# Chunked attention and a multiplicative FFN: the first pair turned by TensorE, its loads split over two queues, and a new order of the opening steps

## The chip, the cores and the metric

The kernel runs on one core of one Trainium2 chip. The metric is the device time of one execution in microseconds (us); the time before is the median of three runs. A profiled execution shows when each engine's instructions ran: TensorE (PE, with its weight loads PEld), VectorE (DVE), ScalarE (ACT), GpSimd (POOL) and SyncE (SP), and the loads and stores that they issue.

## The reference

Inputs q, k, v have the shape (8 batches, 8 heads, 576 positions, 64), in fp32. Attention stays inside chunks of 64 positions; its output feeds a feed-forward part (FFN) of 4608 tokens:

```python
scores = scale * np.matmul(q_c, k_c.transpose(0, 1, 2, 4, 3))      # 64x64 in each chunk
scores = scores - np.max(scores, axis=-1, keepdims=True)
attn = np.exp(scores)
attn = attn / (np.sum(attn, axis=-1, keepdims=True) + 1e-09)
out = np.matmul(attn, v_c)
x = out.transpose(0, 2, 1, 3).reshape(B * S, H * D)                # 4608 x 512
a = x @ w1                                                         # 512 -> 1024
b = x @ w2
h = a * b @ w3                                                     # 1024 -> 1024
return (h @ w_out).astype(np.float32)                              # 1024 -> 512
```

## The kernel before

**Tiling.** Tokens are worked off in 18 "pairs" p of 256 tokens (four chunks of 64); two pairs form a group g of 512 tokens. Everything is computed in bf16 with fp32 sums. The exponentials are taken without subtracting the maximum; at the end a check of the sums decides whether a slow second path has to run (it does not here). The two last matrices are multiplied once, w3·w_out (steps V, W, Z), so that the FFN is (a·b) times one 1024x512 matrix.

**An order written by hand.** The string `ORDER` lists every step of the kernel. The loop at the end of `first_path` runs through it and calls a function for each letter; `inorder` (L90) pins each instruction to its place in its engine's program. So each engine works through its own instructions in the order of the string, and waits for whatever the next of them needs. The steps:

- Loads through GpSimd's queue, cast to bf16 on the way (`load`, L97): `q p`, `k p`, `v p`; `i j`, a quarter of the columns of w1 and of w2; `h j`, a half of w3; `o`, w_out. Eight loads can be in flight; the ninth is issued when the first has landed. A pair whose four chunks lie in two batches is loaded in two pieces (`spans`, L119).
- `R s` (L135): raw fp32 q (s = 0, on SP's queue) and k (s = 1, on ScalarE's queue) of pair 0, in runs of 512 bytes. `K s` (L141): ScalarE casts them to bf16.
- `T p.s` (L195): VectorE transposes q or k of pair p in 32x32 blocks, so that the head dimension lies on the partitions. `G` and `H` (from pair 8 on) put such blocks in place with transfers on SP's queue.
- `S p`, `E p`, `P p` (L214, L231, L238): scores on TensorE, exp on ScalarE, product with v on TensorE. `N p.u` (L258): VectorE takes the reciprocal of the sums and normalises one half (128 tokens) of the pair. `X p.u` (L293): VectorE transposes that half into `xt`, the FFN's input.
- `A p.j`, `B p.j` (L342, L346): the FFN's two first products. For pairs 0 to 3 one such step is 8 matmuls of 256 columns for a quarter j of w1 (A) or w2 (B), so that it needs load `i j` alone. `C p.j` (L349): ScalarE copies A's result out of PSUM. `M p.j` (L353): VectorE multiplies it with B's.
- `V f`, `W m`, `Z m`: w3 transposed by VectorE, multiplied with w_out by TensorE, copied by ScalarE. `O p`, `Y p`, `Q p`: the last product of a pair, its copy and its store.
- `D` (L318): matmuls of zeros that nobody reads: which tile, how many, how many columns. `D0.0.0.16.64` is 16 matmuls of 64 columns; `D0.1.0.4.512` and `D1.0.0.5.512` are four and five of 512 columns, placed between the attention of pairs 0 and 1.

**Buffers.** PSUM is one pool of four tiles of two banks each (`psum`, L100); scores, P's two halves, an A/B step, W and O all take tiles from it, and a tile is free again when its last reader in the order is done (E, N, M, Z or Y). q and k of a pair are one tile of a pool of five; v has six buffers, pair p in buffer p modulo 6.

The opening of the order before the change, up to the first FFN steps:

```
R0 R1 v0 q1 k1 i0 v1 i1 i2 q2 k2 v2 i3 q3 k3 v3 q4 k4 v4 o h0 h1 D0.0.0.16.64 K0 T0.0 K1 T0.1 q5 k5
v5 S0 T1.0 E0 P0 D0.1.0.4.512 T1.1 q6 k6 v6 N0.0 S1 D1.0.0.5.512 X0.0 N0.1 X0.1 A0.0 E1 B0.0 C0.0 P1
```

Of the kernel before, what the change touches and what calls it, by code (L numbers as in the profile page):

```python
# [9 lines left out]
R0 R1 v0 q1 k1 i0 v1 i1 i2 q2 k2 v2 i3 q3 k3 v3 q4 k4 v4 o h0 h1 D0.0.0.16.64 K0 T0.0 K1 T0.1 q5 k5  # L10
v5 S0 T1.0 E0 P0 D0.1.0.4.512 T1.1 q6 k6 v6 N0.0 S1 D1.0.0.5.512 X0.0 N0.1 X0.1 A0.0 E1 B0.0 C0.0 P1
M0.0 A0.1 N1.0 X1.0 B0.1 C0.1 N1.1 A0.2 X1.1 B0.2 C0.2 M0.1 A1.0 T2.0 B1.0 C1.0 M0.2 A1.1 T2.1 q7 k7
v7 B1.1 C1.1 M1.0 S2 M1.1 A0.3 E2 T3.0 B0.3 C0.3 P2 M0.3 A1.2 N2.0 X2.0 B1.2 C1.2 N2.1 A1.3 X2.1
B1.3 C1.3 M1.2 A2.0 T3.1 q8 k8 v8 B2.0 C2.0 M1.3 S3 T4.0 A2.1 E3 M2.0 B2.1 T4.1 q9 k9 C2.1 P3 v9
M2.1 A2.2 N3.0 B2.2 C2.2 X3.0 A2.3 N3.1 B2.3 X3.1 C2.3 M2.2 S4 M2.3 A3.0 E4 B3.0 C3.0 A3.1 M3.0 B3.1
C3.1 V0 A3.2 M3.1 B3.2 C3.2 V1 A3.3 M3.2 B3.3 C3.3 V2 W0 M3.3 V3 W1 Z0 V4 V5 W2 Z1 V6 V7 T5.0 Z2 W3
T5.1 q10 k10 T6.0 T6.1 P4 v10 q11 k11 Z3 S5 N4.0 O0 E5 X4.0 N4.1 X4.1 T7.0 O1 T7.1 Y0 Q0 T8.0 P5 v11
q12 k12 Y1 S6 T8.1 O2 Q1 E6 N5.0 X5.0 N5.1 X5.1 O3 T9.0 T9.1 Y2 G4.0 P6 v12 q13 k13 A4.0 N6.0 B4.0
G4.1 Y3 X6.0 N6.1 C4.0 A4.1 X6.1 B4.1 C4.1 M4.0 Q2 S7 Q3 M4.1 A4.2 E7 T10.0 B4.2 C4.2 T10.1 P7 v13
q14 k14 A4.3 M4.2 B4.3 N7.0 C4.3 A4.4 X7.0 M4.3 B4.4 C4.4 N7.1 A4.5 M4.4 B4.5 C4.5 X7.1 S8 M4.5 S9  # L20
E8 A4.6 T11.0 B4.6 E9 T11.1 P8 v14 q15 k15 C4.6 A4.7 M4.6 G5.0 B4.7 C4.7 N8.0 A6.0 M4.7 B6.0 N8.1
# [12 lines left out]
A12.5 M12.4 B12.5 C12.5 A12.6 M12.5 B12.6 C12.6 A12.7 M12.6 B12.7 C12.7 O9 M12.7 O10 Y9 Q9 A14.0 Y10
B14.0 C14.0 Q10 A14.1 M14.0 B14.1 C14.1 A14.2 M14.1 B14.2 C14.2 A14.3 M14.2 B14.3 C14.3 A14.4 M14.3
B14.4 C14.4 A14.5 M14.4 B14.5 C14.5 A14.6 M14.5 B14.6 C14.6 A14.7 M14.6 B14.7 C14.7 O11 M14.7 O12
Y11 Q11 A16.0 Y12 B16.0 C16.0 Q12 A16.1 M16.0 B16.1 C16.1 A16.2 M16.1 B16.2 C16.2 A16.3 M16.2 B16.3
C16.3 A16.4 M16.3 B16.4 C16.4 A16.5 M16.4 B16.5 C16.5 A16.6 M16.5 B16.6 C16.6 A16.7 M16.6 B16.7
C16.7 O13 M16.7 O14 Y13 Q13 O15 Y14 Q14 O16 Y15 Q15 Y16 Q16 O17
# [7 lines left out]
def first_path(  # L47
# [66 lines left out]
    inorder(nc.vector.memset(zero[:], 0.0))  # L114
    vbuf = [consts.tile([P, 2, H, VW], bf, name=f"vbuf{i}") for i in range(6)]
# [19 lines left out]
    def do_R(s):  # L135

        raw_t[s] = msb.tile([P, H, 2 * D], f32, tag="o_sb", name="raw")
        inorder((nc.sync, nc.scalar)[s].dma_start(
            raw_t[s][:], (q, k)[s][0, :, 0:4 * CH, :].rearrange("h (p t) d -> p h (t d)", t=2)))

    def do_K(s):  # L141
        if 0 not in qk_t:
            qk_t[0] = io.tile([P, 2, H, 2 * D], bf, tag="qk", bufs=5, name="qk")
        inorder(nc.scalar.copy(qk_t[0][:, s], raw_t[s][:]))  # L144
# [19 lines left out]

    def load_v(p):
        for u in range(2):
            for at, b, c, m in spans(4 * p + 2 * u, 2):
                load(vbuf[p % 6][at * CH:(at + m) * CH, u, :, 0:D],
                     v[b, :, c * CH:(c + m) * CH, :].rearrange("h p d -> p h d"))
# [34 lines left out]

    def do_G(g, a):
# [52 lines left out]
    def do_N(p, u):  # L258
# [3 lines left out]
        if u == 0:  # L262
            xn_t[p] = asb.tile([P, 2, 2, 4, D], bf, tag="xn", bufs=3, name="xn")
# [304 lines left out]
```

## Time and profile before

| What | us |
|---|---|
| median of 3 runs (243.94 to 244.39) | 244.36 |
| span of the profiled execution, first to last instruction | 242.9 |
| TensorE busy in it | 226.7 |
| VectorE busy | 154.3 |
| ScalarE busy | 85.2 |
| GpSimd busy (issuing its loads, mostly) | 83.7 |
| first scores matmul (S0) | 9.82 |
| first FFN matmul (A0.0) | 16.57 |
| w3·w_out product done | 65.93 |

The page gives for each engine its busy time and, in 40 slices of the span, its busy share in tenths. A busy TensorE is not one at its peak, since matmuls are pipelined and the ends are modelled. The loads through GpSimd's queue are 18.9 MB in 82,592 packets. A releaser ("<-") behind a wait is the instruction or the transfer that ended it, as semaphore events tell; "issue" is a wait for nothing that the profile shows.

### The profile page before, as it was taken

The page shows a single profiled execution, that of the slowest core. Times are in us where ns is not written, and L with a number is a line of the kernel's source. Part 1 is how long each engine was busy: PE and PEld are TensorE (multiplying, and loading weights), DVE is VectorE, ACT ScalarE, POOL GpSimd, SP SyncE. Part 2 cuts the span into 40 slices and gives each one's busy share as a digit, 9 for nine tenths or more (in the row PEclk, how much of TensorE's full clock was granted, in tenths as well). Part 3 has the DMA queues.
Part 4 walks back from the last instruction along what each step waited for, and adds up shares of the span by engine and source line. Part 5 has one row for each costly group of instructions (what it writes and reads, how often), then busy time and mean ns, then how long its engine had stood idle before and what let it go on. Part 6 is the DMA issues. An engine that isn't in the chain of part 4 may idle for free.

```text
span 242.9 us, 6385 instructions
## 1 busy us (share of the span) xinstructions
PE 226.7 (93%) x2753; PEld 120.2 (49%) x2753; DVE 154.3 (64%) x235; ACT 85.2 (35%) x116; POOL 83.7 (34%) x114
## 2 busy tenths in 40 slices
PE   1189989999999999999999999999999999999994
PEld 1147868874445444444444444444444444444443
DVE  1756799699799588999998899918540332143000
ACT  2412423423333344425336234162332332322322
POOL 7856976656986345764160230000000000000000
PEclk9999999999999999999999999999999999999999
DMA  6999999999999999999999793735502200400244
GB/s 173 179 185 181 185 169 200 196 193 171 167 173 218 222 228 259 179 224 196 205 236 223 221 139 91 163 88 209 142 0 89 87 0 0 173 3 1 86 173 173
DMA packets 93597, 37.65 MB, mean 155 GB/s; under 512 B 75008, under 2 KB 86528, under 8 KB 93568
## 3 DMA queue, kind: packets, MB, share of 16 engines
q0 software_dynamic: 82592, 18.88, 83.9%
q1 hardware_dynamic: 9936, 17.83, 24.0%
q10 hardware_dynamic: 1040, 0.52, 0.8%
q8 instruction: 21, 0.34, 0.6%
q14 instruction: 8, 0.07, 0.1%
HBM read 38.80 MB, written 9.44 MB: 199 GB/s over the span
## 4 chain that ended last, share of the span: by engine, by line
PE 72%; DMA 16%; DVE 4%; SPq 3%; POOL 2%; issue 1%; ACT 0%; DVEq 0%; POOLq 0%
PE ab_ps L95 39%; PE o_ps L95 23%; PE w_ps L95 6%; DMA w<-in_moe_w_dram 4%; DMA qkm<-qkT 3%; SPq L193 3%; DMA qk<-in_q_dram 3%; DMA qk<-in_k_dram 3%; DMA xt<-xm 3%; PE pv L95 2%; PE s_ps L95 2%; DVE qkT L201 2%; POOL vbuf L98 1%; POOL w L98 1%; DVE xt L297 1%
## 5 line engine op out<-in xcount | busy, mean ns | idle before, releaser
L95 PE MATMUL ab_ps<-xt,w 128*128 128x512 bf16 (+1 forms) x688 | 127.4, 342 | 0.7 <-DVE xt L297 0.6
L95 PEld LDWEIGHTS <-w 128*128 128x128 bf16 x704 | 67.1, 98 | 56.1 <-issue 1.8
L366 DVE TENSOR_TENSOR ab<-a_sb,ab_ps 128x512 bf16<-128x512 f32 x71 | 47.8, 674 | 43.4 <-ACT a_sb L351 43.1
L351 ACT COPY a_sb<-ab_ps 128x512 f32<-128x512 f32 x71 | 41.6, 586 | 81.3 <-PE ab_ps L95 81.0
L95 PE MATMUL o_ps<-w3o,ab 128*128 128x512 bf16 (+1 forms) x296 | 63.9, 373 | 0.0
L201 DVE STREAM_TRANSPOSE qkT<-qk 128x1024 bf16<-128x1024 bf16 x36 | 45.1, 1291 | 7.2 <-ACT qk L144 5.5
L95 PEld LDWEIGHTS <-ab 128*128 128x128 bf16 x296 | 28.5, 98 | 32.2
L98 POOL DMA_DIRECT2D vbuf<-in_v_dram x40 | 33.9, 855 | 20.4 <-DMA qk<-in_q_dram 5.2
L396 ACT COPY o_sb<-o_ps 128x1024 f32<-128x1024 f32 x17 | 17.2, 1012 | 45.3 <-PE o_ps L95 41.3
L264 DVE TENSOR_TENSOR xn<-pv,rcs 128x512 bf16<-128x512 f32 x36 | 24.9, 692 | 1.4
L98 POOL DMA_DIRECT2D qk<-in_q_dram x23 | 18.1, 790 | 8.9 <-DMA qk<-in_k_dram 2.4
L98 POOL DMA_DIRECT2D qk<-in_k_dram x23 | 18.0, 783 | 6.5 <-DMA vbuf<-in_v_dram 3.7
L234 ACT ACTIVATE e<-s_ps 128x1024 bf16<-128x1024 f32 x16 | 15.9, 1026 | 1.7 <-PE s_ps L95 1.3
L95 PE MATMUL w_ps<-wo,w3T 128*128 128x512 bf16 x64 | 14.0, 379 | 0.0
L305 DVE STREAM_TRANSPOSE xm<-xn 128x512 bf16<-128x512 bf16 x20 | 13.5, 696 | 0.2
L261 DVE RECIPROCAL rcs<-pv 128x8 f32<-128x8 f32 x36 | 6.9, 193 | 10.4 <-PE pv L95 10.4
L98 POOL DMA_DIRECT2D w<-in_moe_w_dram x16 | 11.1, 695 | 5.3 <-DMA wo<-in_moe_w_out_dram 2.9
L95 PEld LDWEIGHTS <-e 64*32 64x32 bf16 (+1 forms) x832 | 7.8, 97 | 8.7 <-issue 6.9
L95 PE MATMUL pv<-vbuf,e 64*32 64x65 bf16 (+1 forms) x832 | 10.2, 197 | 1.8 <-ACT e L234 1.1
L297 DVE STREAM_TRANSPOSE xt<-xn 128x512 bf16<-128x512 bf16 x16 | 11.4, 711 | 0.5
L389 DVE COPY o_sb<-o_ps 128x256 f32<-128x256 f32 x1 | 0.4, 425 | 16.0 <-PE o_ps L95 16.0
L95 PEld LDWEIGHTS <-qkT 32*64 32x64 bf16 x512 | 5.5, 117 | 10.1 <-DVE qkT L201 7.9
(29 smaller groups left out, 54.2 us busy)
## 6 DMA issues: line engine op xcount, KB each, us to landing
out_dram<-o_sb SPq DMA_DIRECT2D x17, 512.0 KB, 3.3
qkm<-qkT SPq DMA_DIRECT2D x40, 128.0 KB, 4.0
vbuf<-in_v_dram POOLq DMA_DIRECT2D x32, 128.0 KB, 8.2
w<-in_moe_w_dram POOLq DMA_DIRECT2D x16, 256.0 KB, 9.9
qk<-in_q_dram POOLq DMA_DIRECT2D x11, 256.0 KB, 6.8
qk<-in_k_dram POOLq DMA_DIRECT2D x11, 256.0 KB, 7.8
xt<-xm SPq DMA_DIRECT2D x40, 64.0 KB, 3.2
wo<-in_moe_w_out_dram POOLq DMA_DIRECT2D x4, 256.0 KB, 7.1
```

The lines of the kernel that those rows point to most:

```text
L95: return inorder(nc.tensor.matmul(*a, **kw))
L98: return inorder(nc.gpsimd.dma_start(dst, src))
L193: inorder(nc.sync.dma_start(dst, src))
L201: inorder(nc.vector.transpose(qkT_t[g][:, :, p % 2, s, heads(h)].rearrange("p e h (y t) -> p h t e y", t=2), qk_t[p][:, s, heads(h)].rearr ...
L234: inorder(nc.scalar.activation(e_t[p][:, :, heads(hh)], s_t[p][:].rearrange("p u (h q) -> p u h q", q=CH)[:, :, heads(hh)], Exp, scale=sca ...
L261: inorder(nc.vector.reciprocal(rc, pv[:, :, :, D:W]))
L264: inorder(nc.vector.tensor_mul(xn_t[p][:, u], pv[:, :, :, 0:D], rc.to_broadcast([P, 2, 4, D])))
L297: inorder(nc.vector.transpose(new_xt(g)[:].rearrange("p (o t) -> p o t", o=KO)[:, :, t0:t0 + UT] .rearrange("p o (m y) -> p m o y", y=BL), ...
L305: inorder(nc.vector.transpose(xm_t[g][:, u, :, m].rearrange("p o (c y) -> p c o y", y=BL), xn_t[p][:].rearrange("p u r m d -> p (u r) m d" ...
L351: inorder(nc.scalar.copy(a_t[p, j][:], ps_t[p, j][:, 0, :]))
L366: inorder(nc.vector.tensor_mul(o, view(a_t.pop((p, j))[:]), view(ps_t.pop((p, j))[:, 1, :])))
L396: inorder(nc.scalar.copy(o_sb[:], ps_t.pop(p)[:]))
```

## The change

Six things change, and the rest of the kernel stays:

1. The raw q and k of pair 0 are loaded in runs of 1 KB: four positions of a head lie in one partition. Heads 0 to 3 go to partitions 0 to 63 on SP's queue, heads 4 to 7 to partitions 64 to 127 on ScalarE's queue; q first, then k.
2. The cast K is split into two halves, one on VectorE (`K s.0`) and one on ScalarE (`K s.1`).
3. Pair 0's q and k are transposed by TensorE (`t`, 8 transposes of 128x128 for each of q and k, against an identity matrix `eye` that GpSimd makes at the start) into PSUM, and copied out by `u`, two halves for each, one on VectorE and one on ScalarE. T0.0 and T0.1 are gone. Its x is transposed the same way (`y`, 4 transposes for each half, and `z`, a copy on ScalarE); X0.0 and X0.1 are gone.
4. With this layout S0 and P0 are 32 matmuls each (64 before), with 64 rows contracted in each. N0 orders its output for `y` and takes two products of 128x256 for each half.
5. v's buffers are taken from a list: a load takes the buffer that has been given back first, P gives it back.
6. The order is new from its start to about G4.0. In it pairs 0, 1 and 2 have their attention ahead of the first FFN steps (S2 S0 P0 S1 P2, then A0.1 B0.1 A2.1 P1), the loads go q2 k2 q1 k1 v0 v2 i1 v1 i0 q3 k3 i2 v3 i3 h0 o, the FFN steps go by quarters of the weights over three pairs, and only the first of the three groups of zero matmuls (D0.0.0.16.64) is left. From "C4.0 A4.1" on the order is the one of before.

```diff
-R0 R1 v0 q1 k1 i0 v1 i1 i2 q2 k2 v2 i3 q3 k3 v3 q4 k4 v4 o h0 h1 D0.0.0.16.64 K0 T0.0 K1 T0.1 q5 k5
-v5 S0 T1.0 E0 P0 D0.1.0.4.512 T1.1 q6 k6 v6 N0.0 S1 D1.0.0.5.512 X0.0 N0.1 X0.1 A0.0 E1 B0.0 C0.0 P1
-M0.0 A0.1 N1.0 X1.0 B0.1 C0.1 N1.1 A0.2 X1.1 B0.2 C0.2 M0.1 A1.0 T2.0 B1.0 C1.0 M0.2 A1.1 T2.1 q7 k7
...
+R0 R1 q2 K0.0 k2 K1.0 K0.1 D0.0.0.16.64 T2.0 t0.0 K1.1 u0.0.0 t0.1 T2.1 q1 u0.1.0 u0.1.1 T1.0 S2
+u0.0.1 S0 k1 v0 E0 T1.1 P0 v2 S1 N0.0 y0.0 E2 z0.0 i1 N0.1 P2 N2.0 N2.1 y0.1 z0.1 v1 X2.0 X2.1 i0
+A0.1 B0.1 E1 A2.1 P1 N1.0 N1.1 q3 B2.1 A0.0 X1.0 k3 i2 v3 X1.1 B0.0 C0.1 C0.0 M0.0 A2.0 i3 A1.1 M0.1
+T3.0 A1.0 B2.0 B1.0 C2.0 C1.1 B1.1 T3.1 M2.0 S3 C1.0 h0 M1.0 A2.2 C2.1 o E3 B2.2 M2.1 q4 M1.1 C2.2
+P3 A2.3 N3.0 C2.3 B2.3 A1.2 M2.2 A0.2 q5 N3.1 A0.3 X3.1 h1 M2.3 k5 C1.2 X3.0 B1.2 M1.2 V1 A3.1 B3.1
+A3.3 C3.3 V2 q6 C3.1 B3.3 k4 B0.2 V3 M3.1 B0.3 A3.0 M3.3 V0 C0.2 T4.0 B3.0 C0.3 W1 M0.3 A3.2 C3.0
+M0.2 Z1 M3.0 W0 k6 T5.0 v4 V7 A1.3 Z0 C3.2 V6 v5 V4 T5.1 T4.1 q8 W3 V5 Z3 B3.2 q7 k7 M3.2 S5 C1.3 S4
+E4 k8 E5 T6.0 W2 B1.3 T8.0 Z2 v6 T6.1 S6 M1.3 P4 E6 N4.0 O1 N4.1 Y1 P5 v8 X4.0 q9 k9 Q1 v7 v10 T7.0
+X4.1 N5.0 q10 k10 q13 O0 N5.1 T7.1 X5.0 P6 T9.0 Y0 T9.1 T8.1 q11 O3 N6.0 v9 k11 q12 O2 Q0 X5.1 k13
...
+    eye = consts.tile([P, P], bf, name="eye")
+    inorder(nc.gpsimd.affine_select(
+        out=eye[:], in_=zero[:, 0:P], compare_op=mybir.AluOpType.not_equal, fill=1.0, base=0,
+        pattern=[[-1, P]], channel_multiplier=1))
...
-        raw_t[s] = msb.tile([P, H, 2 * D], f32, tag="o_sb", name="raw")
-        inorder((nc.sync, nc.scalar)[s].dma_start(
-            raw_t[s][:], (q, k)[s][0, :, 0:4 * CH, :].rearrange("h (p t) d -> p h (t d)", t=2)))
+        raw_t[s] = msb.tile([P, HH, 4, D], f32, tag="o_sb", name="raw")
+        for g, eng in enumerate((nc.sync, nc.scalar)):
+            inorder(eng.dma_start(
+                raw_t[s][half[g]],
+                (q, k)[s][0, g * HH:(g + 1) * HH, 0:PT, :].rearrange("h (p t) d -> p h t d", t=4)))
...
-        inorder(nc.scalar.copy(qk_t[0][:, s], raw_t[s][:]))
+        x = qk_t[0][:, s].rearrange("p a b -> p (a b)").rearrange("p (t h d) -> p h t d", t=4, h=HH)
+        inorder((nc.vector.tensor_copy, nc.scalar.copy)[j](x[:, 2 * j:2 * j + 2], raw_t[s][:, 2 * j:2 * j + 2]))
...
+    vb_t, vb_free = {}, list(vbuf)
...
+        vb_t[p] = vb_free.pop(0)
...
+    def turn(dst, src):
+        inorder(nc.tensor.transpose(dst, src, eye[:]))
...
+    def do_t(p, s):
+
+        if s == 0:
+            tp_t[p] = ps.tile([P, 2, 2 * 512], bf, tag="p", name="tp")
+        if p == 0:
+            x = qk_t[p][:, s].rearrange("p a b -> p (a b)")
+            for j in range(2):
+                for t in range(4):
+                    turn(tp_t[p][:, s, (4 * j + t) * P:(4 * j + t + 1) * P],
+                         x[:, t * HH * D + j * P:t * HH * D + (j + 1) * P])
+            return
...
+    def do_u(p, s, j=None):
+        if p == 0:
+            inorder((nc.vector.tensor_copy, nc.scalar.copy)[j](
+                turned(p, s)[:, 2 * j:2 * j + 2].rearrange("p i (y t) -> p t i y", t=4),
+                tp_t[p][:, s, 512 * j:512 * (j + 1)].rearrange("p (t i y) -> p t i y", t=4, i=2)))
+            return
...
+    def do_y(p, u):
+        if u == 0:
+            xp_t[p] = ps.tile([P, 2, 2 * 512], bf, tag="p", name="xp")
+        x = xn_t[p][:, u].rearrange("p r m d -> p (r m d)")
+        for o in range(KO):
+            turn(xp_t[p][:, u, o * P:(o + 1) * P], x[:, o * P:(o + 1) * P])
...
+    def do_z(p, u):
+        g, m = divmod(p, 2)
+        t0 = m * PT + u * UT
+        inorder(nc.scalar.copy(new_xt(g)[:].rearrange("p (o t) -> p o t", o=KO)[:, :, t0:t0 + UT],
+                               xp_t[p][:, u, 0:512].rearrange("p (o t) -> p o t", o=KO)))
...
+        if p == 0:
+            qT, kT = turned(p, 0), turned(p, 1)
+            for u in range(2):
+                for i in range(HH):
+                    for b, r in ((0, 0), (1, 1), (0, 1), (1, 0)):
+                        t0, n = (2 * u + r) * CH, (HH * u + i) * CH
+                        mm(s_t[p][half[r], b, n:n + CH], lhsT=kT[half[b], i, t0:t0 + CH],
+                           rhs=qT[half[b], i, t0:t0 + CH], start=True, stop=True)
+            return
```

## The prediction

> **What bounds the kernel now.** I read the busy time by stage first. Cut where the chain of waits turns from loads to matmuls (35.71 us) and where the w3·w_out product ends (65.93 us), with the last 5.7 us of the front shown apart:
>
> ```profile
> 30.00:35.71 5.71, 4.76 (x101) 3.75 (x99) 4.93 (x9) 1.42 (x3) 3.81 (x7) 1.00 2.04 170
> 35.71:52.12 16.41, 16.41 (x321) 14.17 (x322) 13.86 (x20) 6.50 (x10) 10.10 (x15) 1.00 1.47 196
> 52.12:65.93 13.81, 13.81 (x80) 6.15 (x83) 12.62 (x12) 3.63 (x4) 10.00 (x14) 1.00 1.96 174
> 65.93:90.00 24.07, 23.58 (x505) 12.00 (x505) 19.61 (x28) 9.41 (x11) 14.32 (x19) 1.00 1.78 209
> ```
>
> The columns are stretch, length, then busy time of PE, PEld, DVE, ACT, POOL, granted clock, DMA share, GB/s. From 35.71 us TensorE has no idle time at all for 30 us. What PE waited for after 36 us, up to the end, is one line of the view of waits:
>
> ```profile
> PE s_ps L95 <- issue: 0.5, 1, 0.5
> ```
>
> So any microsecond won or lost before about 36 us reaches the end whole, and nothing behind it can be won by an earlier load. The chain of waits says what the front is:
>
> ```profile
> 4.28 6.99 DMA qk<-in_k_dram
> ...
> 11.55 10.19 DMA w<-in_moe_w_dram
> ...
> 23.51 7.11 DMA qk<-in_q_dram
> ...
> 35.71 1.92 PE ab_ps L95 x16
> ...
> 45.03 7.09 PE ab_ps L95 x64
> 52.12 13.81 PE w_ps L95 x64
> ```
>
> Three loads on GpSimd's queue stand one behind the other. That queue's order, and what the engines do with each landing, is what the change rewrites. The timeline shows the price of an unready TensorE:
>
> ```profile
> 9.82 1.07 PE L95 MATMUL z_ps<-qkT 32*64 32x64 bf16 x64 [7.36 <-DVE qkT L201]
> 12.02 0.75 PE L95 MATMUL pv<-vbuf,e 64*32 64x65 bf16 x64 [1.13 <-ACT e L234]
> 12.71 1.89 PE L95 MATMUL z_ps<-zero 128*128 128x512 bf16 x4
> 14.52 1.02 PE L95 MATMUL z_ps<-qkT 32*64 32x64 bf16 x64
> 15.48 1.25 PE L95 MATMUL z_ps<-zero 128*128 128x512 bf16 x5
> 18.51 1.25 PE L95 MATMUL z_ps<-xt,w 128*128 128x256 bf16 x10 [1.12 <-issue]
> ```
>
> Four zero matmuls take 0.47 us each at 12.7 us, five take 0.25 us each at 15.5 us: the array ran at half speed until about 15.4 us, 3.35 us after it became busy without a break at 12.02, although the granted clock is printed as 1.00 throughout. The first FFN matmuls (16.57 us) found it at full speed, thanks to the zero matmuls.
>
> **The change, part by part.** I compare both kernels at one point: all S and P of the first pairs, the 16 FFN steps of pairs 0 to 3 (one A with one B, 16 matmuls, 7.09/4 to 3.60/2, so 1.79 us) and the w3·w_out product done. Before: 65.93 us.
>
> *Loads.* Same bytes, another order: q2 k2 q1 k1 v0 v2 i1 v1 i0 q3 k3 i2 v3 i3 h0 o, where before it was v0 q1 k1 i0 v1 i1 i2 q2 k2 v2 i3. Landings follow one another without a pause (DMA share 1.5 to 2). From one landing to the next: q or k of a pair 1.45 us (30.62 to 32.05), both halves of v 1.75, w1 and w2 of one quarter 2.65 (18.9 to 20.2, twice). The first v landed at 8.75, so the row of landings begins at 8.75 − 1.75 = 7.0. Check: 7.0 + 1.75 + 2.9 + 2.65 = 14.3 for i0, which landed at 14.0. After: q2 8.45, k2 9.9, q1 11.35, k1 12.8, v0 14.55, v2 16.3, i1 18.95, v1 20.7, i0 23.35, q3 24.8, k3 26.25, i2 28.9, v3 30.65, i3 33.3, and wo, as before, at 44.
>
> Two things move that beginning. GpSimd now builds `eye` first, after the zero memset (ends 1.38): 0.10 us by its memset of 128x1, up to 0.9 by one of its DMA issues; I take 0.5, so the first issue comes at about 2.1 instead of 1.50. Against it, raw q and k come in half as many runs and from both hardware queues; they took 5.2 us from issue to landing. The saving is between nothing and about 1 us of the engines' time; I take 0.5, and the two cancel. Ends: −0.7 to +0.9. ScalarE issues two raw loads (0.47 us each) instead of one ahead of its table load (1.28 us, begun at 1.48): about 0.5 us, over long before raw q lands. [...]
>
> *Pair 0 on TensorE.* Removed on VectorE: T0 (2 × 1.30) and X0 (2 × 0.71). Added: four casts of 128x512 and four copies u, half on each engine (ScalarE's copy of 128x512 is 0.59; VectorE's 128x256 0.43, its 128x512 product 0.69; 0.6 taken), z at 0.59, 16 + 8 transposes. A transpose is seen nowhere: 0.055 us by half a 256-column matmul (0.109 apart), 0.27 if nothing overlaps; 0.1 taken while slow. The 16 for q and k lie in the wait for q2 at any of these prices. S0 and P0 drop from 64 to 32 matmuls (0.5 each taken; 0.33 to 1.07). N0 gets two products of 128x256 in place of one of 128x512: 0.2 + 2 × 0.43 = 1.05 (0.9 to 1.6).
>
> *What is queued behind the new waits.* On VectorE T2.0 waits for q2, and u0.0.0, T2.1, u0.1.0, T1.0, T1.1, N0 stand behind it; on TensorE S2 stands ahead of S0. So pair 0's faster load, first by several us, buys nothing: it waits for pair 2. VectorE: T2.0 8.45–9.75, u 10.35, T2.1 11.65, u 12.25, T1.0 13.55, T1.1 14.85, N0.0 (after P0) 15.1–16.15, N0.1 17.2, N2.0/N2.1/X2.0/X2.1 by 20.9. TensorE: S2 11.7–12.8, S0 13.3; E0 14.4; v0 lands 14.55; P0 15.1, S1 16.1, y0.0 16.5; P2 needs the PSUM that N0.1 frees, 17.3–18.0; y0.1 18.4; z0.1 on ScalarE 19.1. i1 has landed at 18.95. **The first FFN step starts at 19.1**, two chains ending 0.2 us apart, so neither shortened alone helps. Before it was 16.57, but with two pairs of attention done, not three.
>
> *From there.* Remaining work: 16 × 1.79 + P1, P3 (2 × 0.63) + S3, S4 (2 × 0.65) + 13.81 = 45.0, so 64.1 if nothing waits. Terms to add:
> (1) The nine zero matmuls D0.1 and D1.0 are gone. From 14.5 to 19.1 PE works about 2.9 of 4.6 us in pieces, where before it took an unbroken 3.35 us. I count the first 3.35 us of FFN at half speed: +1.7 (0 to 3.4). [...]
> (2) A1.1 takes the PSUM that M0.0 frees, and M0.0 waits in VectorE's order behind N1, X1 and C0.0: about 0.5 (0 to 0.8).
> (3) Waits named "issue" in the middle of matmuls stood at 18.51 (1.12) and 31.53 (0.67), after some 450 and 960 TensorE instructions. After, the first falls into the wait before 19.1, the second near S3: +0.7.
> i0 at 23.35 meets A0.0 at 23.3 or later, i2 and i3 are 3 us early, wo comes 3 to 4 us before W1 wants it.
> Sum 64.1 + 1.7 + 0.5 + 0.7 = **67.0, 1.1 us later than 65.93**. Between 52 and 66 us VectorE has six T, four V and three M (7.7 + 5.0 + 2.0 = 14.7 us) against 15 us of TensorE; up to 0.8 us more if they interlock, at nothing here.
>
> Later steps: q13 ahead of q11, three v buffers taken in another order, O1 before O0. PE waited for no load there, so nothing; if that cover were gone, a load is 1.45 us.
>
> The profiled execution spans 242.9; the runs' median, 244.36, is 1.46 above it, taken as unchanged. 242.9 + 1.1 is a span of 244.0 and a time of **245.4**.
>
> **Rivals.**
> B, full speed before the FFN (ends faster). The 2.9 us of small matmuls and transposes count as activity, term (1) vanishes: 65.3, −0.6, 243.7. For it: after 15.5 a pause of 1.12 us did not slow the matmuls. Against: S0 and P0 with pauses of 1.13 between them did not speed up. It decides from more than about half of the 1.7 us.
> C, loads begin earlier. Late in the kernel, on an idle queue, a q took 4.6 us from issue to landing, where the first v took 6.5 for half the bytes: something at the start, the raws or a first use, costs about 2 us. If that goes with the shorter raws, q2 lands near 6.9, both chains move up 1.5 us: −0.4, 243.9. Against: the same 1 MB of raws is there.
> D, slow twice as long (ends later still): a second 3.35 us at half speed, 1.7 more, 247.1. For it: the FFN starts after pieces, not after unbroken work. Against: before, the first unbroken 3.35 us sufficed. [...]
> That the change doesn't do what it says: raw q and k may land no earlier; nothing waits for them, so the time is A's.
>
> **How the numbers follow.** A (245.4) 0.43, B 0.26, C 0.14, D 0.17. Within 0.2% (0.49 us) is about what this measurement cannot tell from no change. A's own range is 244.4 to 246.6; of its 0.43, 0.02 is faster, 0.08 same, 0.33 slower. B splits 0.15, 0.08, 0.03; C 0.08, 0.04, 0.02; D is slower. Sums: faster 0.25, same 0.20, slower 0.55. Range: down to 243.0 (B with better than planned), up to 247.4 (D).
>
> **What would show it.** First ab_ps matmul near 19.1 with z0.1 and i1's landing within 0.5 us before it; its matmuls 0.21 apart instead of 0.11 for 3.35 us; q2 landed near 8.5; T2.0 the longest VectorE wait; the w_ps work ending, S5 and S6 taken off, near 67.0; PE without waits from then on. Wrong if the first FFN matmuls are at full speed, if q2 lands before 7.5, or if PE waits for loads after 40 us.

## The result, and the profile after

The changed kernel takes **258.12 us** (median of 4 runs, 257.54 to 258.35) against 244.26 for the kernel before, run beside it (4 runs, 243.94 to 244.39). The ratio is 1.056, with an interval of 1.0543 to 1.0578: 13.9 us slower. The forecast was 245.4, 1.1 slower. The profiled execution spans 256.0 us, 13.1 more than before.

| | before | forecast | after |
|---|---|---|---|
| first FFN matmul | 16.57 | 19.1 | 26.14 |
| TensorE hardly waits from | 36 | 40 | 58 |
| first o_ps matmul | 67.13 | | 82.06 |
| span | 242.9 | 244.0 | 256.0 |

The page of the changed kernel, its busy shares of TensorE and the granted clock in slices of 6.4 us:

```profile
PE   1345997799999999999999999999999999999994
PEclk9999999589999999999999999999999999999999
```

Two things show at once: TensorE is at most half busy in the first four slices, and in the eighth and ninth the clock falls, which it never did before. The loss by stage (stretch, length, busy time of PE, PEld, DVE, ACT, POOL, granted clock, DMA share, GB/s; the first three lines are one cut, the fourth a stretch by itself):

```profile
26.14:43.01 16.87, 16.06 (x305) 12.95 (x304) 10.42 (x17) 5.65 (x9) 8.72 (x14) 1.00 1.50 195
43.01:57.75 14.74, 11.21 (x79) 8.48 (x74) 7.37 (x12) 1.87 (x5) 8.96 (x13) 0.77 1.66 186
57.75:82.06 24.31, 24.15 (x390) 15.41 (x392) 19.41 (x21) 9.15 (x12) 16.37 (x20) 1.00 1.88 151
...
45.85:52.60 6.75, 6.02 (x28) 4.15 (x28) 1.45 (x3) 1.17 (x2) 4.42 (x7) 0.50 1.53 193
```

From 57.75 on nothing is lost any more; between 43 and 58 us 3.5 us of waits stand beside 6.8 us at half clock. What TensorE waited for, in the view of waits (us in total, times, longest):

```profile
PE tp L216 <- DVE qkT L246: 3.5, 1, 3.5
PE ab_ps L95 <- issue: 2.2, 1, 2.2
PE z_ps L95 <- ACT qkT L246: 2.1, 1, 2.1
PE ab_ps L95 <- ACT a_sb L444: 1.6, 3, 0.7
PE pv L95 <- DVE rcs L347: 1.5, 1, 1.5
...
PE xp L216 <- DVE rcs L347: 1.3, 1, 1.3
...
PE ab_ps L95 <- DVE ab L459: 0.5, 1, 0.5
```

The forecast had two of these: "issue", at 0.7 instead of 2.2, and the 0.5 for M0.0 in the last line. The chain of waits through the opening names the rest (start, length, what):

```profile
9.56 1.09 DVE qkT L211
...
10.77 1.25 DVE qkT L246
12.02 1.14 DVE qkT L211
13.15 1.27 DVE qkT L246
...
14.45 2.44 ACT qkT L246 x2
...
19.52 2.44 DVE xn L354 x2
...
22.02 2.43 DVE xn L354 x2
```

Before, this stretch of the chain was loads. Now it is VectorE and ScalarE: the copies u (L246) and N0's products (L354), 9.8 us of the 16.7 between q2's landing (9.47) and the first FFN matmul. The timeline of TensorE around the second loss:

```profile
42.37 0.70 PE L95 MATMUL pv<-vbuf,e 64*32 64x65 bf16 x64
43.01 0.72 PE L95 MATMUL ab_ps<-xt,w 128*128 128x256 bf16 x5
45.91 0.80 PE L95 MATMUL ab_ps<-xt,w 128*128 128x256 bf16 x3 [2.19 <-issue]
47.38 9.69 PE L95 MATMUL ab_ps<-xt,w 128*128 128x256 bf16 x64 [0.67 <-ACT a_sb L444]
```

64 matmuls of 256 columns take 9.7 us, where before they took 7.1.

### The profile page after: what moved, and what is told of

It is laid out like the page before. It is cut to its first block, busy times and chain, and to the rows that moved or that the text cites. A ratio compares the mean times of both kernels' runs of the same rounds, so it can differ in the third digit from the quotient of the medians.

```text
span 256.0 us, 6280 instructions
## 1 busy us (share of the span) xinstructions
PE 230.3 (90%) x2683; PEld 123.9 (48%) x2704; DVE 156.4 (61%) x237; ACT 87.0 (34%) x120; POOL 84.1 (33%) x115
## 4 chain that ended last, share of the span: by engine, by line
PE 81%; DVE 6%; DMA 4%; ACT 3%; issue 2%; SPq 2%; POOL 0%; DVEq 0%
PE ab_ps L95 46%; PE o_ps L95 24%; PE w_ps L95 5%; PE pv L95 3%; DMA qk<-in_q_dram 3%; PE s_ps L95 2%; SPq L203 2%; DVE xn L354 2%; ACT a_sb L444 1%; DVE qkT L246 1%; ACT qkT L246 1%; DMA qkm<-qkT 1%; DVE qkT L211 1%; DVE xm L398 1%; DVE ab L459 1%
## 5 line engine op out<-in xcount | busy, mean ns | idle before, releaser
L95 PE MATMUL ab_ps<-xt,w 128*128 128x512 bf16 (+1 forms) x698 | 133.5, 348 | 5.4 <-issue 2.2
L95 PEld LDWEIGHTS <-w 128*128 128x128 bf16 x704 | 69.6, 101 | 62.4 <-issue 6.0
L211 DVE STREAM_TRANSPOSE qkT<-qk 128x1024 bf16<-128x1024 bf16 x34 | 42.5, 1288 | 1.8 <-ACT qkT L246 1.4
L357 DVE TENSOR_TENSOR xn<-pv,rcs 128x512 bf16<-128x512 f32 x34 | 23.5, 692 | 1.3
L311 ACT ACTIVATE e<-s_ps 128x1024 bf16<-128x1024 f32 x17 | 16.8, 1028 | 2.7 <-PE s_ps L95 1.4
L95 PE MATMUL w_ps<-wo,w3T 128*128 128x512 bf16 x61 | 14.3, 379 | 0.2
L95 PE MATMUL pv<-vbuf,e 64*32 64x65 bf16 (+1 forms) x800 | 10.6, 200 | 2.7 <-DVE rcs L347 1.5
L500 DVE STREAM_TRANSPOSE w3T<-w 128x1024 bf16<-128x1024 bf16 x8 | 9.5, 1211 | 1.0 <-PE w_ps L95 1.0
L216 PE MATMUL tp<-eye,qk 128*128 128x128 bf16 x16 | 2.2, 306 | 8.4 <-DVE qk L151 4.2
## 6 DMA issues: line engine op xcount, KB each, us to landing
w<-in_moe_w_dram POOLq DMA_DIRECT2D x16, 256.0 KB, 9.4
qk<-in_q_dram POOLq DMA_DIRECT2D x11, 256.0 KB, 6.9
qk<-in_k_dram POOLq DMA_DIRECT2D x11, 256.0 KB, 7.8
wo<-in_moe_w_out_dram POOLq DMA_DIRECT2D x4, 256.0 KB, 10.3
```

The source lines that it names most:

```text
L95: return inorder(nc.tensor.matmul(*a, **kw))
L211: inorder(nc.vector.transpose(qkT_t[g][:, :, p % 2, s, heads(h)].rearrange("p e h (y t) -> p h t e y", t=2), qk_t[p][:, s, heads(h)].rearr ...
L311: inorder(nc.scalar.activation(e_t[p][:, :, heads(hh)], s_t[p][:].rearrange("p u (h q) -> p u h q", q=CH)[:, :, heads(hh)], Exp, scale=sca ...
L357: inorder(nc.vector.tensor_mul(xn_t[p][:, u], pv[:, :, :, 0:D], rc.to_broadcast([P, 2, 4, D])))
L500: inorder(nc.vector.transpose(w3T_t[f][:].rearrange("p k (f y) -> p f k y", y=BL), w3[:, NB * f:NB * (f + 1), :].rearrange("p f (k x) -> p ...
```

## The experiments

Three questions: what made the opening late, what the pause at 43.73 is, and what the half clock costs. The kernel before ran beside each group, at 244.42 to 244.66. Edits of the order are shown as the steps that differ and their neighbours, with line breaks of their own.

### The opening: the order, the turned pair, the writes, the tiles

**The order alone.** The new order, with pair 0 prepared as before (raws, K, T, S, P, N, X of the kernel before):

```diff
-R0 R1 q2 K0.0 k2 K1.0 K0.1 D0.0.0.16.64 T2.0 t0.0 K1.1 u0.0.0 t0.1 T2.1 q1 u0.1.0 u0.1.1 T1.0 S2
-u0.0.1 S0 k1 v0 E0 T1.1 P0 v2 S1 N0.0 y0.0 E2 z0.0 i1 N0.1
+R0 R1 q2 K0 k2 K1 D0.0.0.16.64 T2.0 T0.0 T2.1 q1 T0.1 T1.0 S2
+S0 k1 v0 E0 T1.1 P0 v2 S1 N0.0 X0.0 E2 i1 N0.1
```

> The new order with pair 0 prepared as before (one raw load per tensor, ScalarE's casts, T0, X0, S0 and P0 of 64 matmuls, N0 in one product). Theory: of the 13.9 us about 6 to 7 come from turning pair 0 by TensorE (four copies u of 1.25 us and four products N0 of 1.22 us in one chain up to the first FFN step at 26.14), the rest from the order itself (T2 ahead of pair 0 on VectorE, three pairs first, B behind C, half clock after a pause). Then the first FFN step comes near 22.5 and the time is 250 to 254. Rival, the turn is the whole cost: 244 to 246. Rival, the order is: 256 to 258.

Measured: 255.37 us, ratio 1.0435 (1.0384 to 1.0486), more than the 250 to 254 expected; the first FFN matmul at 23.12. **The turned pair alone**, in the order of before:

```diff
-D0.0.0.16.64 K0 T0.0 K1 T0.1 q5
+D0.0.0.16.64 K0.0 K0.1 t0.0 u0.0.0 u0.0.1 K1.0 K1.1 t0.1 u0.1.0 u0.1.1 q5
...
-X0.0 N0.1 X0.1 A0.0
+y0.0 z0.0 N0.1 y0.1 z0.1 A0.0
```

> The order of before with pair 0 turned by TensorE (split loads, split casts, t, u, y, z, S0 and P0 of 32 matmuls, scattered N0) at the places of K0, T0 and X0, zero matmuls kept. Theory: u and N0 push the first FFN step from 16.57 to about 21.5, of which waits after it take back 1 to 1.5: 247.5 to 249.5. Rival, the order is the whole cost: 244 to 245.5. Rival, the turn is the whole cost: 256 to 258.

Measured: 251.87 us, ratio 1.0292 (1.0242 to 1.0343), more than the 247.5 to 249.5 expected; the first FFN matmul at 24.34. Each part loses by itself, the order 10.7 us and the turned pair 7.2. Together they would lose 17.9; the change loses 13.9. The two can't simply be added, for waits of the one can lie under waits of the other, and the pauses named "issue" fall elsewhere in each: 3.07, 0.91 and 2.54 us with the order alone, 1.31 and 1.08 with the turned pair alone, 2.19 in the changed kernel. How much each of these weighs was not tried. With the order alone the opening held a pause that the changed kernel does not show:

```profile
15.77 0.42 PE L95 MATMUL s_ps<-qkT 32*64 32x64 bf16 x15
19.26 0.86 PE L95 MATMUL s_ps<-qkT 32*64 32x64 bf16 x49 [3.07 <-issue]
```

**Unbroken writes.** u copies a tile as it stands, and N0 normalises as every other pair does; pair 0's positions then stand in another order within its scores, and y picks every fourth feature.

```diff
-                turned(p, s)[:, 2 * j:2 * j + 2].rearrange("p i (y t) -> p t i y", t=4),
-                tp_t[p][:, s, 512 * j:512 * (j + 1)].rearrange("p (t i y) -> p t i y", t=4, i=2)))
+                turned(p, s)[:, 2 * j:2 * j + 2].rearrange("p i y -> p (i y)"),
+                tp_t[p][:, s, 512 * j:512 * (j + 1)]))
...
-            x = xn_t[p][:, u].rearrange("p r m d -> p (r m d)").rearrange("p (o b m z) -> p b m z o", o=KO, b=2, m=HH)
-            for b in range(2):
-                inorder(nc.vector.tensor_mul(x[:, b], ...
```

> The changed kernel with u writing its 512 elements unbroken (the positions of pair 0 then stand in another order in its scores, so pair 0's output is not the reference's) and N0 as one product of 128x512 like all others, y reading every fourth feature. Theory: the copies take 0.6 us instead of 1.25 and an N0 half 0.9 instead of 2.65, 2.6 + 3.5 us less in the chain to the first FFN step, which then starts near 20.2, when i1 has landed (20.0); time 248.5 to 252.5. Rival, these are hidden behind the waits for loads and the later waits decide: 256 to 258.

Measured: 254.8 us, ratio 1.0412 (1.0363 to 1.046), more than the 248.5 to 252.5 expected. Its VectorE timeline has the same copies and products (start, length, operation, idle time before):

```profile
11.16 0.38 DVE L246 COPY qkT<-tp 128x512 bf16<-128x512 bf16 x1
...
12.66 0.41 DVE L246 COPY qkT<-tp 128x512 bf16<-128x512 bf16 x1
...
16.83 0.69 DVE L350 TENSOR_TENSOR xn<-pv,rcs 128x512 bf16<-128x512 f32 x1
```

0.4 instead of 1.25 for u, 0.69 instead of 2.44 for half of N0: the order in which they write made them three times as long. The first FFN matmul came at 22.47, 3.7 us earlier. A pause of 1.82 now stands in S1, ahead of its last matmul: the quicker copies bring TensorE to that place at 17.97, where the changed kernel comes only at 20.4 and does not pause. So the pause took back part of what the writes were worth.

**Tiles apart.** q's and k's transposes get a PSUM tile each and their copies a tile each, and t0.1 stands ahead of u0.0.0, so that no copy waits for another; the writes stay as in the change.

```diff
-        if s == 0:
-            tp_t[p] = ps.tile([P, 2, 2 * 512], bf, tag="p", name="tp")
+        tp_t[p, s] = ps.tile([P, 2, 2 * 512], bf, tag="p", name="tp")
...
-        return (qkT_t[g][:, s, p % 2].rearrange("p b h y -> p (b h y)")
-                .rearrange("p (i t) -> p i t", i=HH))
+        return own[s, 0], own[s, 1]
```

> The changed kernel with t0.1 ahead of u0.0.0 in the order, and separate tiles for what u reads and writes (one PSUM tile for q and one for k, one bank for each half; own SBUF tiles for each half), so that VectorE's and ScalarE's copies need not follow one another; the scattered writes stay. Theory: the copies' waits go, S0 starts near 14.7 instead of 16.9 and the first FFN step near 24: 255.5 to 256.5. Rival, the waits come from the data and not from sharing a tile: 257.5 to 258.5.

Measured: 257.54 us, ratio 1.0524 (1.0402 to 1.0646), from two executions as far apart as 256.38 and 258.69, so the time doesn't say whether 0.6 us was won or nothing; 255.5 to 256.5 was expected. The trace says more: the wait of 3.5 us for u0.0.0 was gone, but z_ps still waited 2.1 us for ScalarE's copies, N0 stayed long, and the first FFN matmul came at 25.90, 0.24 earlier. That copies waited for one another was true, but it was not what set the end of the opening.

**Both in the order of before**, on the run with the turned pair alone:

```diff
-                turned(p, s)[:, 2 * j:2 * j + 2].rearrange("p i (y t) -> p t i y", t=4),
-                tp_t[p][:, s, 512 * j:512 * (j + 1)].rearrange("p (t i y) -> p t i y", t=4, i=2)))
+                turned(p, s)[j][:].rearrange("p i y -> p (i y)"),
+                tp_t[p, s][:, j, 0:512]))
...
```

> The order before, with pair 0 turned by TensorE as in the change, but with unbroken writes in the copies u and in N0's products (pair 0's positions stand in another order in its scores) and with a PSUM tile of their own for q's and k's transposes, so that no copy holds up the next transposes. Theory (the turned pair's loss of 7.2 us in this order is the length of the scattered writes and the copies that wait for one another): u 0.6 instead of 1.25, N0 1.0 instead of 2.6, first FFN matmul near 17, 244 to 246 us. Rival (the loss is the transposes' and ScalarE's place in the order, or the raw loads in 1-KB runs): first FFN matmul at 21 to 24, 250 to 252 us.

Measured: 250.88 us, ratio 1.0264 (1.0238 to 1.029). A miss: the first FFN matmul came at 21.79, not 17. S0 began 1.7 us later than before, because raw k landed later (below); P0 took 1.09 against 0.75, and the five zero matmuls, at half speed, 2.17 against 1.25; and y, z, y, z stand one behind the other ahead of A0.0, where VectorE's X0 had run beside the zero matmuls:

```profile
19.67 0.39 PE L217 MATMUL xp<-eye,xn 128*128 128x128 bf16 x4
20.73 0.38 PE L217 MATMUL xp<-eye,xn 128*128 128x128 bf16 x4 [0.67 <-ACT xt L269]
21.79 1.91 PE L96 MATMUL z_ps<-xt,w 128*128 128x256 bf16 x16 [0.67 <-DMA qk<-in_q_dram]
```

(The last wait is as long as the one for z above it, and the releaser named is a load that A0.0 does not read.) Of the 5.2 us by which the first FFN matmul is late, 1.7 were there at S0 and go with the raw loads; the other 3.5, the half-speed zeros included, come between S0 and A0.0, where pair 0's x is turned. So turning pair 0 on TensorE costs time in that order even with quick copies.

### The raw loads

**Both halves of a tensor on one queue**, still in 1-KB runs:

```diff
-        for g, eng in enumerate((nc.sync, nc.scalar)):
-            inorder(eng.dma_start(
+        for g in range(2):
+            inorder((nc.sync, nc.scalar)[s].dma_start(
```

> The changed kernel, still with raw q and k of pair 0 in runs of 1 KB, but both halves of q on SP's queue and both halves of k on ScalarE's queue. In the run with the order alone, whose raws stand as before (512-byte runs, q on SP's queue, k on ScalarE's), k2 landed at 9.37 and k1 at 12.28; in the changed kernel at 10.6 and 13.31. Theory (it is the split of each tensor over both queues that holds up the loads): k2 and k1 land about 1.1 earlier, raw k by 7.3, the first FFN matmul near 25 and 257 us. Rival (it is the 1-KB runs): landings as in the changed kernel, 258 us.

Measured: 258.32 us, ratio 1.0545 (1.0492 to 1.0598); raw k landed at 9.09 and k2 at 11.23. So the split over queues is not the cause. **Halves of 64 partitions in the kernel before**, with its runs of 512 bytes:

```diff
-        inorder((nc.sync, nc.scalar)[s].dma_start(
-            raw_t[s][:], (q, k)[s][0, :, 0:4 * CH, :].rearrange("h (p t) d -> p h (t d)", t=2)))
+        for g, eng in enumerate((nc.sync, nc.scalar)):
+            inorder(eng.dma_start(
+                raw_t[s][half[g]],
+                (q, k)[s][0, :, 128 * g:128 * (g + 1), :].rearrange("h (p t) d -> p h (t d)", t=2)))
```

> The kernel before, its raw q and k still in runs of 512 bytes and in the same places, but each loaded in two halves of 64 partitions, the first on SP's queue, the second on ScalarE's, as in the change. In the kernel before k and q had landed by 7.3, v0 landed at 8.72 and S0 began at 9.82. Theory (the 1-KB runs, not the halves or the two queues, made the loads about 1 us late in the changed kernel): raw k by 7.6, v0 near 8.8, S0 within 0.3 of 9.8, 244.2 to 244.8 us. Rival (halves of 64 partitions, or two tensors sharing both queues, make them late): raw k at 8.5 or later, v0 near 9.8, S0 near 11, 245 to 246 us.

Measured: 246.17 us against 244.53, ratio 1.0072 (1.0051 to 1.0093). The rival held. Its issues of raw k (KB each, us to landing):

```profile
raw<-in_k_dram ACTq DMA_DIRECT2D x1, 256.0 KB, 7.4
raw<-in_k_dram SPq DMA_DIRECT2D x1, 256.0 KB, 7.7
```

and the first scores in its timeline:

```profile
12.08 1.07 PE L95 MATMUL z_ps<-qkT 32*64 32x64 bf16 x64 [9.61 <-DVE qkT L203]
```

Raw k landed at 9.13 and 9.56 instead of by 7.3, v0 at 9.97 instead of 8.72, and S0 began 2.26 us later (part of it by ScalarE's table load, which now stands behind the wait for raw q, at 6.36 instead of 1.48). Longer runs had nothing to give: ScalarE's queue carried its 0.52 MB in 1040 packets before and in 544 after, and both took 0.8% of the engines' time. So with runs of 512 bytes too the halves made the loads late, raw k by 1.8 us or more. Whether the 64 partitions or the second transfer for each tensor is what costs the time was not tried apart.

### The pause named "issue"

**The middle rewritten**, from P3 to Z2: four steps more (A2.3 B2.3 A1.2 B1.2, 32 matmuls) between S3 and P3, every B ahead of the C of its A.

```diff
-C2.2 P3 A2.3 N3.0 C2.3 B2.3 A1.2 M2.2 A0.2 q5 N3.1 A0.3 X3.1 h1 M2.3 k5 C1.2 X3.0 B1.2 M1.2 V1
+C2.2 A2.3 B2.3 C2.3 M2.2 A1.2 B1.2 C1.2 M2.3 P3 A0.2 M1.2 B0.2 C0.2 N3.0 A0.3 N3.1 B0.3 C0.3 X3.0
...
```

> The changed kernel with the middle of its order alone rewritten, from P3 to Z2: P3's 64 matmuls stand some 178 TensorE instructions behind S3 (6.2 us of work instead of 3.8), and each B step stands ahead of the C step of its A. The front is left as it is. Theory (the pause of 2.19 us at 43.73 comes because S3, two FFN steps and P3 use up 256 TensorE instructions faster than the next 256 are fetched; the pause starts two windows at half clock, which lose 3.0 us; a B behind its own C waits for ScalarE's read of the same PSUM tile): no pause over 1.2 us after 27 us, clock full from 28.7 us on, no wait of 0.67 for a_sb; 2.2 + 3.0 + about 1.3 less, so 251 to 252.5 us, with the first FFN matmul still near 26.1. Rival (the middle waits for loads or for VectorE, and the pause is only where that shows): the wait comes back elsewhere, 256 to 258 us.

Measured: 254.6 us, ratio 1.0409 (1.0379 to 1.0439). From 30.9 to 75.0 us the granted clock stayed at 1.00, and TensorE was busy for 43.22 of these 44.10 us. The first o_ps matmul came at 77.48, 4.6 earlier than in the changed kernel. Two new pauses, of 0.82 in S6 and 1.59 in P5, gave back the difference to the 251 to 252.5 us expected:

```profile
76.63 0.29 PE L95 MATMUL s_ps<-qkT 32*64 32x64 bf16 x12 [0.82 <-issue]
...
83.06 0.31 PE L95 MATMUL pv<-vbuf,e 64*32 64x65 bf16 x29 [1.59 <-issue]
```

This moved much at once. **The changed kernel without its 16 zero matmuls** moves only the count of instructions:

```diff
-R0 R1 q2 K0.0 k2 K1.0 K0.1 D0.0.0.16.64 T2.0 t0.0
+R0 R1 q2 K0.0 k2 K1.0 K0.1 T2.0 t0.0
```

> The changed kernel without its first group of zero matmuls, D0.0.0.16.64: 32 TensorE instructions fewer, in the idle time at the start. Theory (the pause of 2.19 us at 43.73 is the fetch of the next 256 instructions at a fixed count, and it alone starts the two windows at half clock): the count is reached 16 FFN matmuls later, some 2.4 us, by when the fetch is done; no pause of over 0.8 us there, clock full from about 28.7 on, 2.2 + 3.0 us less: 252.5 to 254 us. Rival (the pause belongs to its place, to loads or to buffers, or the zero matmuls do not matter): pause and half clock stay, 257.5 to 258.5 us.

Measured: 254.61 us, ratio 1.0403 (1.0367 to 1.0439), 3.5 us faster for 16 matmuls less in an idle stretch. The same place in its timeline:

```profile
43.62 1.05 PE L95 MATMUL ab_ps<-xt,w 128*128 128x256 bf16 x8
45.34 7.15 PE L95 MATMUL ab_ps<-xt,w 128*128 128x256 bf16 x64 [0.67 <-ACT a_sb L444]
```

No pause, and 64 matmuls in 7.15 us instead of 9.69: the pause was tied to the count, and without it there was no half clock. What the pause waits for stands in the last section: a transfer of instructions. A pause of 1.60 in P5, at 83.20, is why the time is 0.6 above the expected range (252.5 to 254).

The two kernels on the other side. **Before without these zero matmuls:**

```diff
-R0 R1 v0 q1 k1 i0 v1 i1 i2 q2 k2 v2 i3 q3 k3 v3 q4 k4 v4 o h0 h1 D0.0.0.16.64 K0 T0.0
+R0 R1 v0 q1 k1 i0 v1 i1 i2 q2 k2 v2 i3 q3 k3 v3 q4 k4 v4 o h0 h1 K0 T0.0
```

> The kernel before without the first group of zero matmuls, D0.0.0.16.64: 16 matmuls, 32 TensorE instructions fewer ahead of the FFN. They lie in the wait for pair 0's q and k, so they cost no time themselves. Theory (the 'issue' wait of 1.12 us at 18.51 is the fetch of the next 256 instructions, at a fixed count): the count is reached 32 instructions later, behind more FFN work of 0.109 us a matmul, and the wait shrinks or goes: 243.2 to 243.8 us. The second one, 0.67 at 31.53, moves some 1.8 us later and may shrink too. Rival (the wait belongs to that place, the first B step, and not to the count): it stays at 1.1, 244.3 us; if the 16 zero matmuls help the clock, 244.5 to 246.

Measured: 243.71 us (11 runs) against 244.42 (13 runs), ratio **0.9969** (0.9956 to 0.9982): faster than both kernels. The 1.12 at 18.51 went, but the five zero matmuls of D1.0 now ran at half speed (2.23 instead of 1.25) and took nearly all of it back, and the second pause stayed at 0.72:

```profile
15.65 2.23 PE L95 MATMUL z_ps<-zero 128*128 128x512 bf16 x5
17.72 1.91 PE L95 MATMUL z_ps<-xt,w 128*128 128x256 bf16 x16
```

So the size was as expected and the reason only in part: at 35.6 us it was 0.1 ahead, and it was 0.8 ahead only past 88 us, where the third pause (0.49 at 87.72) had gone too. Its profiled execution was the longest of its eleven (245.42), with a wait for a transfer at 145 us that the kernel before does not have. **Before with 64 instead of 16:**

```diff
-h0 h1 D0.0.0.16.64 K0 T0.0
+h0 h1 D0.0.0.64.64 K0 T0.0
```

> The kernel before with 64 zero matmuls of 64 columns in its first group instead of 16: 96 TensorE instructions more, in the idle time at the start, where they cost nothing themselves. Theory (a pause falls where 256 instructions are used up sooner than the next 256 are fetched, 6 to 7 us in this stretch): the count now falls into S1, some 4.7 us after the one before it, so TensorE pauses there for 1.5 to 2.3 us; the 1.12 at 18.51 and probably the 0.67 at 31.53 go; the zero matmuls behind S1 start cold and some of the first FFN runs at half speed: 244.5 to 247 us. Rival (zero matmuls at the start do not matter, or help the clock): 243.5 to 244.4 us, pause at 18.5 as before.

Measured: 249.91 us, ratio 1.0223 (1.0186 to 1.0259). The first pause fell where it was expected, after 27 matmuls of S1, with 0.86 us instead of 1.5 to 2.3; those of before (1.12, 0.67 and 0.49) went, but three others came, the longest 2.10 us behind 51 matmuls of S6. More was lost than the 0 to 2.5 us expected, 5.4 us, for 48 matmuls in an idle stretch. In the profiled execution, 4.8 us slower, the four pauses make 5.2 us against 2.3 before, and the zero matmuls and FFN matmuls behind S1 lose 1.9 by half speed:

```profile
14.46 0.58 PE L95 MATMUL z_ps<-qkT 32*64 32x64 bf16 x27
15.90 0.70 PE L95 MATMUL z_ps<-qkT 32*64 32x64 bf16 x37 [0.86 <-issue]
16.53 2.31 PE L95 MATMUL z_ps<-zero 128*128 128x512 bf16 x5
```

### The clock at the first FFN step, and all parts mended

**Zero matmuls in TensorE's waits** ahead of A0.1, on the kernel with the rewritten middle:

```diff
-S0 k1 v0 E0 T1.1 P0 v2 S1 N0.0 y0.0 E2 z0.0 i1 N0.1 P2
+S0 k1 v0 E0 T1.1 D0.1.0.2.512 P0 v2 S1 N0.0 D2.2.0.3.512 y0.0 E2 z0.0 i1 N0.1 D2.2.0.3.512 P2
```

> The changed kernel with the middle rewritten (as in e5_middle), and eight zero matmuls of 512 columns put into TensorE's waits ahead of the first FFN step: two between S0 and P0, three ahead of y0.0, three ahead of P2. Theory (the first FFN steps run at half speed because what comes before them is broken by waits of 1.1 to 1.5 us): TensorE is busy nearly without a break from 17.4 us, the clock is full before 26 us, the first 24 FFN matmuls take 2.6 us instead of 5.06, and the time falls by 1.5 to 2.5 from 254.6: 252.1 to 253.1 us. Rival (pieces that short do not keep the clock, or the zero matmuls hold up the path): first FFN matmuls still at half speed or later than 26.5, 254.5 to 256 us.

Measured: 253.65 us, ratio 1.0363 (1.0329 to 1.0398):

```profile
25.59 2.78 PE L96 MATMUL ab_ps<-xt,w 128*128 128x256 bf16 x24 [0.67 <-ACT xt L271]
```

24 matmuls in 2.78 us, against 4.03 in the changed kernel and 5.06 in the run it was built on. 1.0 us of the 1.5 to 2.5 expected reached the end; a pause of 1.87 at 72.95 and a stretch of half clock behind it took the rest.

**All of it mended**: the changed kernel with unbroken writes, tiles apart and t0.1 first, and the rewritten middle, every B ahead of its C:

```diff
-T2.0 t0.0 K1.1 u0.0.0 t0.1 T2.1
+T2.0 t0.0 K1.1 t0.1 u0.0.0 T2.1
...
-C2.2 P3 A2.3 N3.0 C2.3 B2.3 A1.2 M2.2 A0.2
+C2.2 A2.3 B2.3 C2.3 M2.2 A1.2 B1.2 C1.2 M2.3 P3 A0.2
...
-                tp_t[p][:, s, 512 * j:512 * (j + 1)].rearrange("p (t i y) -> p t i y", t=4, i=2)))
+                tp_t[p, s][:, j, 0:512]))
```

> The changed kernel with all of it mended: unbroken writes, transposes of q and k in tiles of their own and ahead of the copies, the middle rewritten as in e5_middle, every B ahead of its C. What is left is its order of loads with three pairs ahead of the FFN, and the FFN's start after broken work. Theory: first FFN matmul near 21.3, about 4.8 later than before against one pair of attention more done (1.5), half speed at its start, one fetch wait in S1 or P2: 247 to 249.5 us, so still slower than before: the order of the opening is the rest of the loss. Rival (the mended parts were the whole loss): 243 to 245.5 us.

Measured: 252.34 us, ratio 1.0329 (1.0299 to 1.0358): above the 247 to 249.5 expected, and 7.9 us behind the kernel before. The chain and the waits show where: pauses of 1.99 in S1, 1.67 and 1.31 at S6 and P5, 1.25 for a quarter of the weights, half speed in the first 24 FFN matmuls (4.04 against 2.78). These five sum to 7.5 us. The execution they were read from is the fastest of the four (251.00, its span 6.6 us longer than before's), and the kernel before has 2.3 us of such pauses of its own, so this lists losses and is no balance:

```profile
PE s_ps L95 <- issue: 3.7, 2, 2.0
...
PE pv L95 <- issue: 1.3, 1, 1.3
PE ab_ps L95 <- DMA w<-in_moe_w_dram: 1.2, 1, 1.2
```

No kernel with the new order and without these pauses was run; that it would then equal the kernel before is arithmetic, not shown.

## Why the prediction was wrong

The side was right, the size was not. By its own steps, taken at the first o_ps matmul (82.06 after; 67.13 before plus 0.64 for S6, which the new order puts ahead of it: 14.3 us late):

| step | forecast | measured | difference |
|---|---|---|---|
| sum against before | +1.1 | | 1.1 |
| first FFN step | 19.1 | 26.14 | 7.0 |
| (1) half speed at its start | 1.7 | 4.03 − 2.78 = 1.25 | −0.4 |
| (2) PSUM waits | 0.5 | 0.52 + 0.29 + 2 × 0.67 = 2.15 | 1.6 |
| (3) "issue" pause | 0.7 | 2.19 | 1.5 |
| half clock behind it | none | (9.69 − 7.15) + (0.80 − 0.33) = 3.0 | 3.0 |
| sum | | | 13.8 |

0.5 us have no place; behind 82 us the changed kernel won back 1.2. The terms are those of the profiled execution. In the other three the granted clock over the span was 0.992 or 0.993 instead of 0.987, which by estimate is one stretch of 3.4 us at half clock instead of two (3.4 × 0.5 of 256 us is 0.007), and they were no faster (258.11 to 258.35): where they lost the time instead isn't known.

*First FFN step: the step that failed.* Copies u were priced at 0.6 by unbroken rows of the same size, and N0's products at 0.43 by a copy of 128x256; they took 1.22 to 1.30 and 1.22, for their scattered writes (shown by the unbroken run: 3.7 us). The forecast's bounds, 0.9 to 1.6 for half of N0, did not hold the 2.65 measured, because no row with such writes was sought for the upper end. It also let VectorE's and ScalarE's u run side by side. In the trace they stand one behind the other, but setting them apart brought the first FFN matmul forward by 0.24 us only. The loads were the second piece: q2 at 9.47 and k2 at 10.6 instead of 8.45 and 9.9. With the order alone and whole raws k2 landed at 9.37, so the working of the landings was right and "half as many runs save up to 1 us" wrong: it overlooked the halves. A third piece shows once the writes are quick, the pause of 1.82 in S1. By estimate these three are all: the unbroken run's 22.47, less its pause and 1.4 for its loads (q2 at 9.86 instead of 8.45), is 19.25, near the 19.1. One reading of the opening was wrong without a price: ScalarE's table load was to be over before raw q lands, but it began only at 5.96, behind the wait for raw q (at 1.48 before); the copies of pair 0 wait for q2 anyway.

*The clock.* Term (1) was right in kind; rival B fell. The size of term (1) was near by luck: with the same opening, the run with the rewritten middle lost 5.06 − 2.78 = 2.28 us there instead of 1.25. No run shows the 3.4 us at the upper end of its range; these 2.28 are the most that was lost there. Rival D's price, a second half-speed stretch, came true at another place: not at the start but behind the pause at 43.73.

*The "issue" pause* was found in the trace of before and carried over as 0.7, "near S3"; the place was right. What was missed is how soon the 256 instructions before it were used up: S3, two FFN steps of 8 matmuls and P3 did that in 3.8 us. Taking P3 four steps further from S3, or 16 idle matmuls away, brings the first o_ps matmul 4.6 us earlier.

*PSUM waits.* The 0.52 for M0.0 was forecast. Not forecast: with C ahead of B in the new order, B's matmuls wait for ScalarE's read of the tile that they share with A, 0.29 and twice 0.67. In the run with each B first in the middle only the 0.29 is left.

*Later.* "PE waits for no load after 40 us" held; nor did the order of q13, v or O cost anything. That the change does not do what it says held for the raws: raw k landed later, not earlier.

## What to carry to other kernels

Price an operation by a row with the same pattern of writes, not only the same size, and a transfer split into halves of 64 partitions by a row of such halves (raw k landed 1.8 us or more later with them). Bursts of small matmuls can use up instructions faster than they are fetched (64 matmuls with their weight loads, half a block, took 0.64 us; from the count before a pause to the pause's own, a whole block, 3.7 to 7.2 us went by, the pause included): count TensorE's instructions along the order, keep such bursts apart, and before removing or adding idle matmuls see where the counts then fall. A pause of about two microseconds costs itself and, in some cases, half clock behind it: 2.19 and 3.0 us in the changed kernel.

## What the runs showed of the hardware

**Where TensorE pauses.** In the records of all fifteen kernels, the 34 pauses of TensorE named "issue" and longer than 0.25 us stand at the same counts of matmuls: after 223, 478, 605, 734, 987 or 988, 1114 to 1116, 1244, 1371 or 1372 and 1499, whatever stood there. These are 223 and multiples of 128 behind it, up to five short. In the kernel before the first is 16 + 64 + 64 + 4 + 64 + 5 + 6 = 223; with 64 zero matmuls it is 64 + 64 + 64 + 4 + 27 = 223. A matmul with its weight load is two instructions, so 128 are 256. The page of before shows what arrives:

```profile
PE 226.7 (93%) x2753; PEld 120.2 (49%) x2753; DVE 154.3 (64%) x235; ACT 85.2 (35%) x116; POOL 83.7 (34%) x114
...
q8 instruction: 21, 0.34, 0.6%
```

5506 instructions, 21 transfers of 16 KB; in the run with 64 zero matmuls 5602 and 22. In the traces each of the 34 pauses ends 1.2 to 1.7 us after such a transfer has ended: in the changed kernel one ran from 43.55 to 44.49 and TensorE went on at 45.91; in the kernel before one ran from 16.23 to 17.18 and TensorE went on at 18.51. None of the first eleven counts was passed sooner than 1.2 us after its transfer, in any kernel, and where it had ended long before there was no pause. So, by these traces, the pause is the wait for the next block of instructions; the 34 took 0.3 to 3.1 us. The 42 transfers in the kernels before and after took 0.9 to 1.6 us each. What varies is when it begins: for these 34, 1.4 to 4.4 us after TensorE passed the count before, so that from one count to the next 3.7 to 7.2 us went by, the pause included. What sets that beginning was not tried.

**Which pause lowers the clock** its length alone does not say. Half clock followed pauses of 2.19, 2.26, 2.29 and 2.54 us, 1.87 and 1.59; it did not follow those of 1.31 and less, nor another of 1.59, nor 1.60, 1.67, 1.79 and 2.10. (The pauses of 1.82, 1.99 and 3.07 in the opening are left out: there the matmuls ran at half speed before them too, with the granted clock printed as 1.00.) Its stretches lasted 3.4 or 6.8 us; the one in the changed kernel, which two expectations call two windows, lasted 6.8. What decides beside the length was not tried.

**Scattered writes.** VectorE's copy of 128x512 took 1.25 us in the changed kernel, with steps of 8 bytes in its output, and 0.38 unbroken, in the run with unbroken writes; ScalarE's 1.22 and 0.54; the product of 128x512 2.44 in two parts with steps of 256 bytes and 0.69 unbroken.
